# A linear-attention and MLP kernel whose first 520 entries are ordered by a written list

## The chip, the cores and the metric

The kernel runs on one core of one Trainium2 chip. The metric is device time in microseconds (us), from the start of the program to its end, as the median of several runs. A profile is one execution of it, taken by the hardware profiler.

## The reference

Two blocks follow one another. The first is linear attention with a decay per head, in blocks of 64 tokens; the second is a two-layer MLP with a leaky ReLU.

```python
batch, n_heads, seq, head_dim = (4, 8, 768, 64); block = 64
for b in range(nb):
    qb, kb, vb = (q[:, :, sl], k[:, :, sl], v[:, :, sl])
    intra = np.einsum('bhic,bhjc->bhij', qb, kb) * Dmask[None]      # lam**(i-j), lower triangle
    intra = np.einsum('bhij,bhjd->bhid', intra, vb)
    inter = np.einsum('bhid,bhde->bhie', qb * lam_pow[None], kv_state)
    out[:, :, sl] = intra + inter
    kb_dec = kb * rev_pow[None]
    kv_state = lam_block[None, :, None, None] * kv_state + np.einsum('bhsd,bhse->bhde', kb_dec, vb)
# x: (3072 tokens, 512)
h = x @ w_in            # 512 x 2048
g = np.maximum(0.01 * h, h)
return (g @ w_out).astype(np.float32)   # 2048 x 512
```

q, k, v and lam are float32. w_in and w_out are float64.

## The kernel before

**Tiling.** A chunk is 128 tokens (two blocks of 64) of one batch entry, all 8 heads; there are 24 chunks, six for each batch entry. Four chunks make a group of 512 tokens; there are six groups. The hidden width of 2048 is cut into eight units of 256. `up(g, p)` computes unit p of the first layer for group g; `down(g, p)` adds two units of the second layer.

**Precision by three products.** Every operand of the MLP is split into three fp32r parts h, l and m (`xh`, `xl`, `xm` and `wh`, `wl`, `wm`). A block of `up` is h x h products, l x l products, a scaling of the bank by ScalarE (L658), m x m products, and a leaky ReLU by ScalarE into `gs` (L661), which is stored to DRAM. Each product of 128 features is four matmuls (L640).

**float64 by hand.** `to_float32` (L566 to L585) loads half a unit of w_in as 64-bit words into one of three `raw` buffers; ScalarE makes three passes over it (L578, L580, L582), VectorE a shift (L584) and an add (L585). `parts` then makes `wh` (L591 on ScalarE or L593 on VectorE), `wl` (L596) and `wm` (L602).

**A chunk of attention.** k and q are loaded (L338) and v (L388); TensorE transposes k and q (L403); ScalarE copies the transposes out (L414, L415); k is scaled by the decay (L419, on GpSimd from chunk 2 on); q is scaled (L423, on VectorE for chunks 0 to 3, on GpSimd after); scores and the k-v products go into `psc` by quadrant matmuls (all through L313); VectorE masks the scores (L452) and updates the state (L457, L459), which GpSimd multiplies by lambda (L462); then `own` and two `inter` groups of matmuls go into `po`, with a small read of `po` between (L491), and ScalarE and VectorE split the result into `xh` (L507), `xl` (L508) and `xm` (L510).

**Order.** The functions only record operations with an engine, an assumed time and the buffers read and written (`Plan.add`). `seq` at the end of the kernel gives the rank. `Plan.emit` then simulates the engines by assumed times, takes at every step the operation that can start first, and emits all in that order. Each engine runs its own queue in order; all of the loads and stores named here are issued by SyncE. In gaps that the plan sees on TensorE before the bank `b10` is first used, `emit` calls `busy`, which adds filler transposes (L266); nine more stand at the start.

**Banks.** Four PSUM banks are used beside `psc` and `po`: `pt` for q's transposes, `b11` for k's transposes of the first four chunks, `b10` and `b2` (and later `b11`) for `up`. Which one a block of `up` gets is fixed by a counter.

## Time and profile before

| | |
|---|---|
| median of 3 runs | 610.32 us (610.25 to 611.13) |
| the profiled execution | 610.55 us |
| its span | 608.8 us |
| TensorE matmuls busy | 598.1 us |
| VectorE busy | 313.4 us |
| ScalarE busy | 269.1 us |
| GpSimd busy | 86.2 us |
| TensorE clock granted, mean | 0.999 |
| DMA read and written from HBM | 68.69 and 35.65 MB |

The span is the time from the first to the last instruction of the profiled execution; its own time is 1.75 us more. PE is TensorE's matmuls, PEld its weight loads, DVE is VectorE, ACT ScalarE, POOL GpSimd, SP SyncE. A row of a timeline gives the start, the duration, the engine, the line of the code, the operation, the output and the inputs, and the number of instructions. A row of the table by form gives the busy sum, the mean of one in ns and the idle time in front. The filler transposes count as busy.

### The profile page before, as it was taken

Reading aid. Unit: us, or ns where it says so; the run is one execution under the profiler, and the core shown is the slowest. Engines: PE = TensorE matmul, PEld = TensorE weight load, DVE = VectorE, ACT = ScalarE, POOL = GpSimd, SP = SyncE. Lnnn points to the kernel's source line nnn. Section 1 sums busy time; section 2 is a strip of 40 time slices with the busy share of each in tenths; the row PEclk is TensorE's granted clock in tenths of the full one; section 3 lists DMA queues with packets and bytes.
Section 4 is the critical chain, followed back from the end, with each engine's and each line's share of the span. In section 5 each row is a group of like instructions: output and inputs, shape, how many; then the busy total and the mean of one; then the engine's idle time right before and its main releaser. Section 6 shows DMA issues by size and latency. Waiting matters only on the chain.

```text
span 608.8 us, 12931 instructions
## 1 busy us (share of the span) xinstructions
PE 598.1 (98%) x5386; PEld 495.0 (81%) x5386; DVE 313.4 (51%) x418; ACT 269.1 (44%) x430; POOL 86.2 (14%) x90
## 2 busy tenths in 40 slices
PE   7799999999999999999999999999999999999997
PEld 6678888888888878888788888888888888888886
DVE  5899764334243426326366755545454554635531
ACT  4678974434455646555577522222222313214111
POOL 1654412105133004104000000000000000000000
PEclk9999999999999999999999999999999999999999
DMA  9999774667888878786686843524333333433201
GB/s 209 235 261 272 210 202 122 175 149 187 200 208 239 214 229 207 212 253 216 228 300 219 288 145 103 173 69 139 138 104 129 114 136 106 139 104 122 86 1 69
DMA packets 147754, 105.18 MB, mean 173 GB/s; under 512 B 123632, under 2 KB 124400, under 8 KB 147696
## 3 DMA queue, kind: packets, MB, share of 16 engines
q1 hardware_dynamic: 147408, 104.29, 58.6%
q8 instruction: 42, 0.69, 0.5%
q14 instruction: 16, 0.13, 0.1%
q10 hardware_dynamic: 288, 0.07, 0.0%
HBM read 68.69 MB, written 35.65 MB: 171 GB/s over the span
## 4 chain that ended last, share of the span: by engine, by line
PE 94%; DMA 2%; DVE 2%; ACT 1%; issue 0%; DVEq 0%; SPq 0%; ACTq 0%
PE b L640 42%; PE b L700 18%; PE po L700 11%; PE psc L700 11%; PE po L313 4%; PE psc L313 4%; PE pt L700 4%; DMA g<-gs 1%; DMA att<-in_v_dram 1%; PE pt L403 1%; DMA att<-in_k_dram 1%; PE po L403 0%; DVE wm L602 0%; ACT att L415 0%; DVE wl L596 0%; ACT gs L661 0%
## 5 line engine op out<-in xcount | busy, mean ns | idle before, releaser
L682 ACT ACTIVATE xh<-att 128x1024 fp32r<-128x1024 f32 x48 | 50.7, 1060 | 148.7 <-PE b L700 140.7
L683 DVE SCALAR_TENSOR_TENSOR xl<-att,xh 128x1024 fp32r<-128x1024 f32 x48 | 58.6, 1223 | 98.0 <-ACT xh L682 98.0
L640 PE MATMUL b<-xm,wm 128*128 128x512 f32 (+2 forms) x392 | 104.5, 392 | 0.3 <-ACT b L658 0.3
L640 PE MATMUL b<-xh,wh 128*128 128x512 f32 (+2 forms) x392 | 103.5, 387 | 0.8 <-ACT xh L507 0.8
L640 PE MATMUL b<-xl,wl 128*128 128x512 f32 (+2 forms) x392 | 103.3, 387 | 0.0
L640 PEld LDWEIGHTS b<-xh,wh 128*128 128x128 f32 x392 | 72.8, 188 | 16.5 <-ACT xh L507 0.9
L640 PEld LDWEIGHTS b<-xl,wl 128*128 128x128 f32 x392 | 72.7, 188 | 14.9 <-DVE wl L596 0.2
L640 PEld LDWEIGHTS b<-xm,wm 128*128 128x128 f32 x392 | 71.4, 188 | 15.6 <-ACT b L658 0.8
L658 ACT ACTIVATE b<-b 128x512 f32<-128x512 f32 (+2 forms) x97 | 55.9, 579 | 58.9 <-PE b L640 58.7
L661 ACT ACTIVATE gs<-b 128x512 f32<-128x512 f32 (+2 forms) x97 | 56.9, 592 | 44.5 <-PE b L640 37.9
L700 PE MATMUL b<-wh,xh 128*128 128x512 f32 x192 | 74.7, 389 | 0.0
L700 PE MATMUL b<-wl,xl 128*128 128x512 f32 x192 | 74.7, 389 | 0.0
L685 DVE SCALAR_TENSOR_TENSOR xm<-xl,xh 128x1024 fp32r<-128x1024 f32 x48 | 58.7, 1225 | 4.7
L462 POOL TENSOR_TENSOR att<-att 128x256 f32<-128x256 f32 x40 | 35.0, 874 | 57.6 <-DVE att L459 57.6
L700 PEld LDWEIGHTS b<-wl,xl 128*128 128x128 f32 x192 | 36.0, 187 | 7.5
L700 PEld LDWEIGHTS b<-wh,xh 128*128 128x128 f32 x192 | 36.1, 188 | 7.4
L452 DVE TENSOR_TENSOR att<-psc,att 128x512 f32<-128x512 f32 x24 | 16.5, 689 | 42.1 <-PE psc L313 42.0
L423 POOL TENSOR_TENSOR att<-att 128x512 f32<-128x512 f32 (+1 forms) x20 | 24.6, 1228 | 95.7 <-DVE att L383 46.8
L700 PE MATMUL psc<-wm,xm 128*128 128x512 f32 (+1 forms) x100 | 37.9, 384 | 0.0
L700 PE MATMUL psc<-wh,xh 128*128 128x512 f32 x96 | 37.3, 389 | 0.0
L700 PE MATMUL psc<-wl,xl 128*128 128x512 f32 x96 | 37.3, 389 | 0.0
L700 PE MATMUL po<-wh,xh 128*128 128x512 f32 x96 | 37.3, 389 | 0.0
(73 smaller groups left out, 784.9 us busy)
## 6 DMA issues: line engine op xcount, KB each, us to landing
att<-g SPq DMA_DIRECT2D x48, 512.0 KB, 3.2
g<-gs SPq DMA_DIRECT2D x47, 512.0 KB, 4.0
raw<-in_moe_w_in_dram SPq DMA_DIRECT2D x16, 512.0 KB, 5.1
raw<-in_moe_w_out_dram SPq DMA_DIRECT2D x16, 512.0 KB, 4.8
att<-in_k_dram SPq DMA_DIRECT2D x48, 128.0 KB, 4.1
att<-in_v_dram SPq DMA_DIRECT2D x24, 256.0 KB, 4.5
out_dram<-gs SPq DMA_DIRECT2D x23, 256.0 KB, 2.2
wo<-w SPq DMA_DIRECT2D x8, 512.0 KB, 5.7
```

The lines of the kernel that those rows point to most:

```text
L313: nc.tensor.matmul(dst[HALF[cols]], lhsT=lhsT[HALF[rows]], rhs=rhs[HALF[rows]], start=start, stop=True, skip_group_check=True)
L403: nc.tensor.transpose(out=at[y], in_=src[:, 2 * y:2 * y + 2, :].rearrange("p a d -> p (a d)"), identity=ident)
L423: add(eng, us, lambda: e.tensor_tensor(o, x, _bc(pow_q, 2, 2)[:, :, m, :], op=ALU.mult), ["fq", dep], [f"qsT{i}"])
L452: add("DVE", 0.69, lambda: nc.vector.tensor_tensor(sc, psc[:, :, lower, :], decay, op=ALU.mult), ["psc", "fk"], ["sc"])
L462: add("POOL", 0.7, lambda new=new, j=j: nc.gpsimd.tensor_tensor(state[(j + 1) % 4], new, _bc(lam_c, 2, D), op=ALU.mult), [f"st{j % 4}", "f ...
L640: nc.tensor.matmul(dst, lhsT=w[z][:, kk * 2 * P + f * P:kk * 2 * P + (f + 1) * P], rhs=x[z][:, kk, toks], start=start and kk == 0, stop=kk ...
L658: add("ACT", ns, lambda b=b: nc.scalar.activation(out=b, in_=b, func=AF.Copy, bias=0.0, scale=S + 1.0), [], [kb], rank=-1.5)
L661: add("ACT", ns, lambda b=b, r=r: nc.scalar.activation(out=r, in_=b, func=AF.Prelu, bias=0.0, scale=1.0 / WS, alpha=0.01), [kb], [f"gs{jg} ...
L682: add("ACT", 1.05, lambda: nc.scalar.activation(out=h, in_=graw[j], func=AF.Copy, bias=0.0, scale=NEAR), reads, wr("h"))
L683: add("DVE", 1.25, lambda: nc.vector.scalar_tensor_tensor(l, graw[j], 1.0, h.bitcast(F32), op0=ALU.mult, op1=ALU.subtract), reads + [f"rh{ ...
L685: add("DVE", 1.25, lambda: nc.vector.scalar_tensor_tensor(m, l.bitcast(F32), -S, h.bitcast(F32), op0=ALU.mult, op1=ALU.add), [f"rh{j}", f" ...
L700: nc.tensor.matmul((to if z == 2 else acc[tb][0])[:, cols], lhsT=ring[j][z][:, f * T + tb * P:f * T + (tb + 1) * P], rhs=W[pp][z][:, f * d ...
```

## The change

- **The list.** `ORDER` names 520 entries: an operation by its number in order of recording, and the engine that it goes to (t TensorE, s ScalarE, v VectorE, g GpSimd, d DMA). These are emitted in the listed order, and the rest by the planner as before. A negative number stands for that many fillers; there are eight of these in all, after the nine at the start, and none are added in gaps.
- **Names given late.** `Slot` objects stand for a bank, a `raw`, `low` or `gs` buffer; `Plan.resolve` gives each the free buffer of its kind that ended longest ago in the program. The banks `pt`, `b11`, `b10` and `b2` thus rotate over the transposes of k (first four chunks) and q, the k-v products of the first four chunks (which leave `psc`), and `up`.
- **q by pairs.** q of chunks 0 to 5 is loaded by three pairs of chunks; partition p holds tokens 2p and 2p+1, so that a packet is 512 bytes instead of 256. The pair is transposed by 32 matmuls of 64 x 64 into two banks; copies and scalings put the tokens back in order, the scaling of q by halves.
- **Scratch.** k, v of chunks 2 and 3 are loaded into the two `gs` buffers, q of chunks 2 and 3 into `raw2`.
- **First two units in halves.** `up(0,1)` and `up(0,0)` are each cut into chunks 0, 1 and chunks 2, 3.
- **Engines.** q's scaling is on VectorE for chunks 0 to 7, k's on either engine for chunks 0 to 7; copies of the transposes of the first four chunks may go to VectorE.
- **The planner** also gets other assumed times, and keeps VectorE's SBUF-only operations apart from GpSimd's (`lock`). `LOW_PE` and `MIX_PE` are empty, so their branches are not taken.

In recording order the entries begin with 0 to 2 the decay factors; chunk 0 is 3 to 25 (3 load k, 4 load the q pair, 5 load v, 6 and 7 transposes, 8 and 9 copies, 10 scale k, 11 scale q, 12 scores, 13 k-v, 14 mask, 15 and 17 state, 19 own, 20 and 22 inter, 23 to 25 xh, xl, xm); 26 to 47 chunk 1, 48 to 71 chunk 2, 72 to 93 chunk 3; 94 to 108 unit 1 of w_in (106 wh, 107 wl, 108 wm); 154 to 161 the first half of `up(0,1)` (159, 160 its m products); 247 wl of unit 3; 275 l products of `up(0,3)`.

```diff
+    ORDER = [(int(x[:-1]), ENGINE[x[-1]]) for x in (
+        "4d 3d -5t 7t 9s 5d 94d 26d -2t 6t 8s 12t 0v 2v 1v 14v 10g 13t 15v 11v 19t 20t 16g 96s 95s 30s 98v 17v 18g 28t 27d 31v 35t 32v 29s 21s 97s 48d 22t 23s "
+        "37v 51t 99v 33v 24v 34t 36v 41t 42t 38g 39v 25v 100d 53v 102s 101s 104v 49d 52t 43v 55g 103s 105v 54s 56v 57v 50d 163d 44t 59t 72d 73d 110d 169d 109d "
+        "58t 45s 106s 154t 40g 61v 62g 46v 60v 74t 107v 77g 65t 66t 165s 76s 75s 78v 63v 79v 155t 81t 164s 167v 82v 67s 166s 68t 69s 170s 171s 80t 156t 157t "
+        "64g 83v 84g 70v 87t 88t 113t 89s 158s 90t 91s 108v 47v 173v 85v 92v -1t 159t 160t 187t 112t 111d 225d 120d 119d 168v 115s 172s 174v 161s 114s 175s "
...
+    APART = 4
+    LOW_PE, MIX_PE = set(), set()
+    PAIRS = {"q": {0, 1, 2}}
+    QS = 8
+    KM = 8
...
+    def load_pair(nm, c):
+        b, n, i = of(c)
+        y, (dst, keys) = (q if nm == "q" else k)[b, :, n * C:(n + 2) * C, :], pair(nm, c)
+        def go():
+            for z in range(2):
+                nc.sync.dma_start(out=dst[:, z * HP:(z + 1) * HP].rearrange("p h s d -> p h (s d)"),
+                                  in_=y[z::2].rearrange("h (p s) d -> p h (s d)", s=2))
+        move(1.75, go, [], keys, issue=1.0, name=f"{nm}{c}")
...
+        def go_pair(nm, ats):
+            src = pair(nm, c)[0]
+            for y in range(HP):
+                for s in range(2):
+                    for x in range(2):
+                        for a in range(2):
+                            quad(ats[x][y][:, s * C2:(s + 1) * C2], x, src[:, 2 * y + a, s, :], ident[:, HALF[x]], a, start=y == 0 and s == 0)
...
+                for t in range(1 if n == 0 else 0, 2):
+                    add("DVE", 0.41, lambda t=t: scale_pair(t), ["fq"] + dep, [f"qsT{i}"])
...
+        kp = [Slot("bank") for _ in range(n_pu)] if apart else ["psc"] * n_pu
...
+    def resolve(self, program):
...
+                if s.name is None:
+                    able = [x for x in self.kinds[s.kind] if holds[x] is None or not holds[x].left]
+                    s.name = self.kinds[s.kind][s.fixed] if s.fixed is not None else min(able, key=lambda x: ended[x])
...
+        for i, e in self.order:
+            if i < 0:
+                done.append((free[e], len(done), i, e))
+                free[e] -= 0.11 * i
+                continue
+            take(max(free[e], since(i, e)), i, e)
...
-    seq = [("a", 0), ("a", 1), ("a", 2), ("a", 3), ("wi", 1), ("b", 4), ("r", 4), ("up", 0, 1), ("wi", 0), ("r", 5),
-           ("wi", 2), ("wi", 3), ("up", 0, 0), ("up", 0, 2), ("up", 0, 3), ("r", 6), ("up", 1, 1, 0, 3), ("r", 7),
+    seq = [("a", 0), ("a", 1), ("a", 2), ("a", 3), ("wi", 1), ("b", 4), ("r", 4), ("up", 0, 1, 0, 2), ("wi", 0), ("up", 0, 0, 0, 2), ("up", 0, 1, 2, 4), ("r", 5),
+           ("wi", 2), ("wi", 3), ("up", 0, 0, 2, 4), ("up", 0, 2), ("up", 0, 3), ("r", 6), ("up", 1, 1, 0, 3), ("r", 7),
```

## The prediction

> **What bounds the kernel now.** I read the page first: the busy shares and the chain that ended last.

> ```profile
> span 608.8 us, 12931 instructions
> ...
> PE 598.1 (98%) x5386; PEld 495.0 (81%) x5386; DVE 313.4 (51%) x418; ACT 269.1 (44%) x430; POOL 86.2 (14%) x90
> ...
> PE 94%; DMA 2%; DVE 2%; ACT 1%; issue 0%; DVEq 0%; SPq 0%; ACTq 0%
> ```

> TensorE is both the busiest engine and the chain. So the change can pay only where TensorE does nothing useful. The table by stretches shows where that is:

> ```profile
> 0.00:10.00 10.00, 7.84 (x106) 6.31 (x110) 4.94 (x21) 2.85 (x4) 1.08 (x8) 1.00 0.90 173
> 10.00:20.00 10.00, 8.18 (x264) 6.65 (x257) 7.87 (x14) 7.13 (x15) 4.56 (x6) 1.00 1.03 246
> 20.00:30.00 10.00, 7.68 (x215) 5.95 (x214) 8.58 (x13) 6.56 (x12) 6.84 (x7) 1.00 0.94 245
> 30.00:40.00 10.00, 9.54 (x104) 7.32 (x103) 9.24 (x13) 6.99 (x13) 5.84 (x5) 1.00 0.99 272
> 40.00:50.00 10.00, 10.00 (x152) 8.27 (x151) 9.62 (x14) 9.21 (x18) 3.28 (x3) 1.00 0.86 225
> ```

> Columns: stretch, length, then PE, PEld, DVE, ACT, POOL busy, granted clock, DMA share, GB/s. PE gaps end near 32 us. After that the waits of PE list only 0.34 us at 223 and 0.28 us at 298. Before it, busy PE holds fillers. DMA is full and DVE climbs to 9.6 of 10. I therefore asked which DVE operations run longer than their shortest, over 0 to 56 us by form:

> ```profile
> L585 DVE CUSTOM_DVE_ANT_0 w<-w,low 128x1024 uint16<-128x1024 uint16 x8 | 7.4, 925 | 0.6
> L584 DVE TENSOR_SCALAR w<-w 128x512 int32<-128x512 int32 x8 | 5.9, 734 | 0.0
> L596 DVE SCALAR_TENSOR_TENSOR wl<-wh,w 128x1024 fp32r<-128x1024 f32 x4 | 5.6, 1406 | 0.0
> L452 DVE TENSOR_TENSOR att<-psc,att 128x512 f32<-128x512 f32 x7 | 4.8, 688 | 2.9 <-PE psc L313 2.9
> L602 DVE SCALAR_TENSOR_TENSOR wm<-wl,wh 128x1024 fp32r<-128x1024 f32 x3 | 4.4, 1472 | 0.0
> L593 DVE TENSOR_SCALAR wh<-w 128x1024 fp32r<-128x1024 f32 x3 | 2.8, 940 | 0.1
> ```

> The forms that read only SBUF are stretched. Undisturbed rows of the same lines are 0.69 (L585, L593), 0.42 (L584) and 1.22 us (L596, L602). The excess is 1.9+2.5+0.7+0.8+0.7 = 6.6 us. L452, which reads PSUM, stays at 0.69. POOL is stretched too: L462 takes 0.62 us alone and up to 1.62.

> **A common mark.** I compare both kernels where the fourth unit, up(0,3), starts its l products. DVE's timeline has the end of the wl that it needs:

> ```profile
> 53.98 1.55 DVE L596 SCALAR_TENSOR_TENSOR wl<-wh,w 128x1024 fp32r<-128x1024 f32 x1
> ```

> and PE's the last chunk round before it and the mark itself, start and duration:

> ```profile
> 49.90 0.60 PE L403 MATMUL po<-att 128*128 128x128 f32 x4
> 50.34 0.60 PE L403 MATMUL pt<-att 128*128 128x128 f32 x4
> 50.87 0.93 PE L313 MATMUL po<-att 64*64 64x64 f32 x48
> 51.62 1.11 PE L313 MATMUL psc<-att 64*64 64x64 f32 x64
> 52.55 0.41 PE L313 MATMUL po<-att 64*64 64x64 f32 x16
> ...
> 56.65 1.98 PE L640 MATMUL b<-xl,wl 128*128 128x512 f32 x8
> ```

> From start to start these price TensorE: k and q transposes of a chunk 0.97, own and first inter 0.75, scores 0.93, second inter 0.34. A full product (4 matmuls of 512 columns) is 0.907, of 384 columns 0.70 (63.62 to 64.32); so 256 columns are 0.907 - 2 x 0.21 = 0.485, an estimate.

> DVE reaches the mark's input (end of wl for up(0,3)) at 55.53. It starts at 3.44 when lam lands. Its rows up to there, at undisturbed durations, sum to 42.3 us. So 52.1 - 42.3 = 9.8 us are lost: idle 6.5 (1.6, 2.1, 1.4, 0.8, 0.4, 0.2 by stretch), excess 6.6, less about 3.4 won because neighbours overlap (36.45 to 37.05 is 0.60 for a 0.68 us row).

> **The change, part by part.**

> *Listed order, DVE.* In the list 70 DVE entries stand up to that same wl. At the rows' durations: factors 3.2, six sc 4.1, eleven state steps 4.5, q scalings 5.2, two k scalings 1.3, eight shifts 3.4, eight adds 5.5, five xl 3.4, four xm 2.8, two heads 1.4, four wl 4.9, three wm 3.7, a copy and a peek 0.8: 44.2 us. That is 1.9 more than before, mainly q scalings that POOL had. So wl ends at 3.44 + 44.2 + loss = 47.6 + loss.

> *Loads.* Six loads of 256 KB landed from 4.55 (k of chunk 0) to 10.26 (v of chunk 1: issued 6.16, 4.1 to landing): 1.14 us each. A q pair has 512 KB in packets twice as long; no row shows these. Bounds are 1.14 (time goes by packets) and 2.28 (by bytes); I take 1.75, as w_in's 512 KB, with longer packets, lies in between. In list order this lands q of chunks 0 and 1 at 5.2, k0 6.3, v0 7.4, the first half of unit 1's w_in 9.1, k1 10.3, v1 11.4, k2 12.6, the second half 14.3. SyncE also gets the first G store ahead of the loads of unit 3's w_in. It waits for a leaky ReLU near 29; the row of such loads (6.2 us to landing at 31.81) still puts them ahead of their use near 45.

> *Walk to unit 1's third part.* k0 transposed 6.9, copied by ACT 7.6, scores 8.2; DVE idle 6.7 to 8.4. That first half's shift waits for two ACT passes (0.8 idle), the first state step for v1 and scaled k1 (0.4). With these 2.9 us (rest 0) the 21.7 us of DVE entries up to chunk 1's xm end at 28.0. Excess adds 1.2, overlap takes 1.8: 27.4. Then PE starts the m products at 27.5, against 35.38 before (there for four chunks, here for two).

> *Rest of the DVE loss.* Idle from 27 to the mark: before 1.4, take 2.0 for more joints. Excess in all: POOL had 18.8 us of work by undisturbed rows (7 k scalings of 1.06, 11 state steps of 0.62, 4.6 of q scalings) and is left 11.5, so 6.6 x 11.5/18.8 = 4.0 if the disturbance goes with POOL's work, 0 if the order avoids all; I take 2.4, nearer the row. Overlap -3.6. Sum of losses: 2.9 + 2.0 + 2.4 - 3.6 = **3.7**, bounds 0 to 9.8. [...]

> *TensorE.* A pair's q is transposed by 32 quadrant matmuls, half of the 64 in a 0.93 row: 0.47 in place of 0.97. Bounds 0.47 and 0.97. Three pairs: -1.5. Two units in halves: 24 x 0.485 - 12 x 0.907 = +0.8. From the m products to the mark the list has 22.8 us of PE work (35.8 less 13.0 by these prices). Before, 20.25 us of work took 21.27 (35.38 to 56.65), 5% more. So PE could be there at 27.5 + 22.8 x 1.05 = 51.4. DVE gives 47.6 + 3.7 = 51.3. The two agree, so neither alone yields more.

> *Fillers.* All idle fillers go but eight. They lie where PE waits, so their removal is priced at 0 while the clock holds.

> *Rotating banks, sums in a bank of their own, moved scratch.* They free waits on buffers: PE waits after 75 us are 0.6 in all, so at most 0.6 is won there, and I take 0. The greedy part after entry 520 has new costs; 0, bounds -0.6 to +2.

> *Sum.* At the mark the list has two products of 0.907 not yet done. Equal state comes at 51.4 + 1.8 = 53.2, against 56.65: 3.4 us gained. Profiled execution: 610.55 (span 608.8 and 1.75 around it), 0.23 above the median of 610.32. Forecast: 610.55 - 3.4 = 607.1 profiled, **606.9** median. In general the gain is 7.1 less DVE's loss. What 0.2% (1.2 us) can't tell from none lies between 609.1 and 611.5.

> **Rivals.**

> *Loads land sooner and the order avoids POOL.* Pair and weight halves at 1.14: v1 lands 1.2 earlier, idle falls by it, excess to 0: loss 0.1. PE is then at the m products by 25 and gives 3 more than now at most: 604. For: the entries after each state step read mostly PSUM. Against: queues drift from a plan. 0.18.

> *DVE loses what it lost before (slower).* Loss 9.8 gives 7.1 - 9.8 = -2.7: **613.0**. It decides from a loss of 7.1 up, at the mark's wl. For: more DVE entries, a fixed order that waits for its slowest load, DMA share already 1.0; and if each POOL entry blocked DVE for its whole 11.5 us, the loss would be 12.8 and the time 616.3. Against: POOL has 40% less work, and 6.6 of its 18.8 us disturbed DVE before. 0.17, of it 0.07 slower than 611.5, 0.05 within, 0.05 short of it.

> *TensorE's clock falls without fillers (slower).* The first nine fillers took 2.18 us, 0.24 each; later two take 0.44 (11.62) and five 0.76 (25.22), 0.11 for each more: a slow pace exists. About 5 us of PE steps lie on the walk; at 2.2 times they add 6: 612.9. Against: all stretches before show 1.00, with waits up to 1.4, and my walk's longest is 1.4. [...] 0.05.

> *The later, greedy part opens waits,* on banks or stores, of 2 us: 609. 0.08.

> *The list fixes order, not times:* if a pair costs 2.28, the first lands 0.5 later and the gain is 2.9; inside the forecast.

> **How the numbers follow.** Forecast 0.52 (605.2 to 608.7, loss 2 to 5.5). Faster: 0.52 + 0.18 + 0.05 + 0.04 = 0.79. Within: 0.05 + 0.03 = 0.08. Slower: 0.07 + 0.05 + 0.01 = 0.13. The range 603.2 to 610.6 leaves out the slower cases and the end of the first rival.

> **What would show it.** Right: m products of unit 1 near 27.5, wl of up(0,3) ending near 51, l products there soon after, L584 to L602 stretched by under 4 us in all before it, PE clock 1.00 from 10 us on, no PE wait over 0.5 after 75 us. Wrong: DVE idle over 5 us between 7 and 28, or PE waiting on DVE rows between 30 and 60.

## The result, and the profile after

The change is slower: 612.48 us (median of 10, 611.69 to 615.6) against 610.69 us for the kernel before beside it (10 runs, 610.17 to 612.28). The ratio is 1.0035, 95% interval 1.0018 to 1.0052. The forecast was 606.9, range 603.2 to 610.6. The profiled execution after took 614.3 us (span 612.5), 1.8 above its own median; before's took 610.55 (span 608.8).

The page of the kernel after, the busy row and the chain:

```profile
span 612.5 us, 13328 instructions
...
PE 599.5 (98%) x5589; PEld 499.9 (82%) x5589; DVE 309.2 (50%) x429; ACT 264.4 (43%) x429; POOL 77.0 (13%) x85
...
q8 instruction: 44, 0.72, 0.5%
...
PE 91%; DMA 4%; ACT 1%; issue 1%; SPq 1%; DVE 0%; DVEq 0%; ACTq 0%
```

TensorE has 203 more matmul records than before, and 4.9 us more of weight loads. The "q8 instruction" row, which I had not used, is the DMA queue that brings the instructions: 44 packets, 0.72 MB, so 16 KB each. The table by stretches, kernel after (length, PE, PEld, DVE, ACT, POOL, granted clock, DMA share, GB/s):

```profile
0.00:10.00 10.00, 7.25 (x168) 6.14 (x172) 4.15 (x20) 2.93 (x4) 1.80 (x8) 1.00 0.82 194
10.00:20.00 10.00, 6.52 (x243) 5.25 (x237) 7.35 (x16) 5.43 (x11) 4.68 (x5) 0.95 1.09 264
20.00:30.00 10.00, 8.04 (x244) 7.18 (x240) 9.27 (x17) 6.97 (x12) 3.44 (x5) 0.84 1.08 276
30.00:40.00 10.00, 10.00 (x232) 9.73 (x228) 6.13 (x9) 7.28 (x14) 1.72 (x2) 0.87 0.59 146
```

Two things stand against the rows of before. The clock is no longer 1.00, and VectorE's share at 30 to 40 us fell from 9.2 to 6.1: it waits. The timelines say for whom, first PE's, then DVE's (kernel after):

```profile
13.79 0.21 PE L428 MATMUL b<-att 64*64 64x64 f32 x1 [0.77 <-issue]
...
18.90 0.21 PE L428 MATMUL pt<-att,raw 64*64 64x64 f32 x1 [0.95 <-issue]
...
28.86 0.70 PE L871 MATMUL pt<-xl,wl 128*128 128x256 f32 x4 [1.96 <-issue]
...
32.54 0.66 PE L428 MATMUL po<-att 64*64 64x64 f32 x16
...
33.22 1.20 PE L871 MATMUL pt<-xm,wm 128*128 128x256 f32 x8
...
56.99 1.07 PE L871 MATMUL b<-xl,wl 128*128 128x512 f32 x4
```

```profile
4.05 0.24 DVE L398 COPY att<-att 128x4 f32<-128x4 f32 x2 [4.05 <-DMA att<-in_lam_dram]
...
33.87 0.69 DVE L718 TENSOR_TENSOR xl<-po,xh 128x512 fp32r<-128x512 f32 x1 [4.01 <-ACT xh L710]
...
54.33 1.23 DVE L829 SCALAR_TENSOR_TENSOR wl<-wh,w 128x1024 fp32r<-128x1024 f32 x1
```

"issue" means that the engine waited for nothing the profile shows: no buffer, no semaphore, no data. Counting all of TensorE's instructions in the trace (matmuls, weight loads and a few of its sequencer), these waits stand at instructions 450, 706 and 1218, the first two in the middle of a transposed q pair, and 450, 706, 962, 1218 are 256 apart: TensorE gets its instructions in blocks of 256 (16 KB / 256 = 64 bytes each). Its 11228 instructions pass 44 such places (194 + 256k), and the row has 44 packets; in the kernel before 10818 pass 42, with 42 packets. By the DMA records, each wait ends 1.3 to 1.4 us after the end of an instruction packet. In the kernel before the same boundaries passed at 15.36, 18.81, 24.82 and 34.47 us with no such wait, the one at 18.81 only just (1.3 us after its packet's end). VectorE then waits 4.01 us for an xh, which ScalarE makes from a chunk's output that TensorE had late (its last products started at 32.54), and the wl of up(0,3) ends at 55.56 (55.53 before), with two products of 0.907 us still to do at the mark (56.99).

### The profile page after: what moved, and what is told of

It reads as the page before. It is cut to its first block, busy times and chain, and to the rows that moved or that the text cites. A ratio compares the mean times of both kernels' runs of the same rounds, so it can differ in the third digit from the quotient of the medians.

```text
span 612.5 us, 13328 instructions
## 1 busy us (share of the span) xinstructions
PE 599.5 (98%) x5589; PEld 499.9 (82%) x5589; DVE 309.2 (50%) x429; ACT 264.4 (43%) x429; POOL 77.0 (13%) x85
## 4 chain that ended last, share of the span: by engine, by line
PE 91%; DMA 4%; ACT 1%; issue 1%; SPq 1%; DVE 0%; DVEq 0%; ACTq 0%
PE b L871 29%; PE b L938 18%; PE pt L871 11%; PE psc L938 11%; PE po L938 11%; PE po L428 4%; PE pt L938 4%; PE psc L428 3%; DMA g<-gs 2%; DMA wo<-w 1%; DMA raw<-in_moe_w_in_dram 1%; DMA raw<-in_moe_w_out_dram 1%; PE b L428 1%; PE b L564 0%; PE po L564 0%
## 5 line engine op out<-in xcount | busy, mean ns | idle before, releaser
L871 PE MATMUL b<-xm,wm 128*128 128x512 f32 (+3 forms) x296 | 77.2, 386 | 0.7 <-ACT b L896 0.7
L871 PE MATMUL b<-xh,wh 128*128 128x512 f32 (+3 forms) x296 | 76.5, 381 | 0.0
L871 PE MATMUL b<-xl,wl 128*128 128x512 f32 (+3 forms) x296 | 76.4, 380 | 0.0
L871 PEld LDWEIGHTS b<-xl,wl 128*128 128x128 f32 x296 | 54.2, 188 | 11.0 <-DVE xl L718 0.5
L871 PEld LDWEIGHTS b<-xh,wh 128*128 128x128 f32 x296 | 54.1, 188 | 10.6
L871 PEld LDWEIGHTS b<-xm,wm 128*128 128x128 f32 x296 | 52.8, 188 | 11.6 <-ACT b L896 1.3
L896 ACT ACTIVATE b<-b 128x512 f32<-128x512 f32 (+2 forms) x71 | 41.2, 581 | 41.6 <-PE b L871 41.6
L899 ACT ACTIVATE gs<-b 128x512 f32<-128x512 f32 (+1 forms) x71 | 41.6, 590 | 39.0 <-PE b L871 35.6
L655 DVE TENSOR_TENSOR att<-psc,att 128x512 f32<-128x512 f32 x24 | 16.5, 688 | 50.3 <-PE psc L428 50.2
L665 POOL TENSOR_TENSOR att<-att 128x256 f32<-128x256 f32 x40 | 29.5, 737 | 82.7 <-DVE att L662 52.3
L817 DVE TENSOR_SCALAR w<-w 128x512 int32<-128x512 int32 x32 | 15.3, 480 | 46.5 <-ACT w L811 46.5
```

The source lines that it names most:

```text
L655: add("DVE", 0.685, lambda: nc.vector.tensor_tensor(sc, psc[:, :, lower, :], decay, op=ALU.mult), ["psc", "fk"], ["sc"])
L665: add("POOL", 0.62, lambda new=new, j=j: nc.gpsimd.tensor_tensor(state[(j + 1) % 4], new, _bc(lam_c, 2, D), op=ALU.mult), [f"st{j % 4}", " ...
L817: add("DVE", 0.42, lambda: nc.vector.tensor_scalar(d, d, 3, None, op0=ALU.logical_shift_left), [], [key], lock=True)
L871: nc.tensor.matmul(dst, lhsT=w[z][:, kk * 2 * P + f * P:kk * 2 * P + (f + 1) * P], rhs=x[z][:, kk, toks], start=start and kk == 0, stop=kk ...
L896: add("ACT", ns, lambda b=b: nc.scalar.activation(out=b(), in_=b(), func=AF.Copy, bias=0.0, scale=S + 1.0), [], [kb], rank=-1.5)
L899: add("ACT", ns, lambda b=b, r=r: nc.scalar.activation(out=r(), in_=b(), func=AF.Prelu, bias=0.0, scale=1.0 / WS, alpha=0.01), [kb], [kg], ...
```

## The experiments

Every variant was timed over five rounds beside the kernel before, which had a median of 611.01 to 611.61. Numbers of the table: ratio to before with interval; start of unit 1's m products, end of the wl of up(0,3), and TensorE's waits for "issue" in the first 60 us, all three from one profiled execution, in us. Before: 35.38, 55.5, none; after: 33.22, 55.6, 3.8. In the quoted expectations S and F are one theory, that TensorE lacks its own instructions; B adds that the packets stand behind queued data. C is the halved clock in e1 to e7; in e9 to e11 it is that a packet takes a time of its own.

| run | ratio (95%) | m products | wl end | issue |
|---|---|---|---|---|
| e1 no pairs | 1.0029 (1.0017 to 1.0041) | 31.9 | 54.1 | 0.2 |
| e5 no pairs, 26 fillers | 1.0026 (1.0010 to 1.0043) | 28.7 | 51.0 | 2.9 |
| e17 the same again | 1.0026 (1.0010 to 1.0042) | 30.3 | 52.5 | 2.3 |
| e6 pairs, 26 fillers | 1.0053 (1.0036 to 1.0070) | 35.8 | 58.1 | 6.7 |
| e9 e5, q of chunk 8 later | 1.0007 (0.9992 to 1.0021) | 28.9 | 51.6 | 2.7 |
| e10 e9, store ahead of W4 | 1.0009 (0.9996 to 1.0022) | 29.9 | 52.7 | 1.8 |
| e11 e10, W4 held | 1.0029 (1.0014 to 1.0043) | 29.6 | 51.7 | 1.4 |
| e12 one pair (4, 5), 26 fillers | 0.9998 (0.9982 to 1.0014) | 29.9 | 52.3 | 1.5 |
| e15 the same again | 1.0019 (1.0005 to 1.0033) | 32.1 | 55.3 | 2.2 |
| e13 e12 with e10's loads | 1.0030 (1.0013 to 1.0048) | 31.5 | 53.8 | 2.6 |
| e16 the same again | 1.0040 (1.0014 to 1.0066) | 32.9 | 56.3 | 2.8 |
| e14 one pair (0, 1), 26 fillers | 1.0018 (1.0004 to 1.0032) | 32.4 | 56.1 | 1.9 |

**No pairs (e1).**

```diff
-    PAIRS = {"q": {0, 1, 2}}
+    PAIRS = {"q": set()}
```

with the list's numbers moved to match; the two q loads of a pair stand where the pair's stood.

> The changed kernel with q of chunks 0 to 5 loaded, transposed and scaled chunk by chunk again, each entry at its place in the list: 24 matmuls in place of 96 for these transposes, so 144 fewer TensorE instructions (a weight load and a matmul each). Theory S (TensorE waits for its own instructions, which come in blocks of 256, about 5 us apart in the first 30 us): the waits at 13.8, 18.9 and 28.9 us shrink or vanish, 610.5 to 611.7, that is 0.8 to 2 faster than the change. Theory L (the pair loads with longer packets are what helps the start): every early load is later, 613.5 to 615. Theory C (only the halved clock costs): within 0.5 of the change, unless the clock also stays up.

The instruction waits are gone (0.2 us), but the time stayed near the change's (1.0029 against 1.0035), so theory S missed its gain of 0.8 to 2 us. The run has 168 matmul records fewer, 336 instructions with their weight loads and not 144. The granted clock fell instead (10 to 20 us, then 20 to 30, kernel e1):

```profile
10.00:20.00 10.00, 7.72 (x168) 5.99 (x160) 6.81 (x15) 5.56 (x10) 4.68 (x5) 0.65 0.90 220
20.00:30.00 10.00, 9.71 (x278) 8.42 (x280) 7.54 (x13) 7.00 (x12) 3.80 (x4) 0.84 1.02 231
```

**Long fillers (e2).** Three fillers of 512 columns were listed at two waits of the change.

```diff
+        if n > 100:
+            for _ in range(n - 100):
+                nc.tensor.matmul(bank[at][:, 0:T], lhsT=ident, rhs=_bc(ident, 1, 4), start=True, stop=True, skip_group_check=True)
+            return
```

> The changed kernel with three more fillers of few instructions: one matmul of 512 columns ahead of chunk 1's own products (where TensorE waits from 15.6 to 16.5 us) and two ahead of the l product that starts at 28.9 us. They keep TensorE busy in both 3.4 us windows that came before a half-speed window, with 6 more instructions. Theory C: no half-speed window up to 60 us, time 610.8 to 611.6. Theory S: the instruction waits stay, though the clock holds: 612 to 613 (gain under 0.5).

614.37, ratio 1.0045 (1.0029 to 1.0062). The fillers did not fill this wait, being instructions too: two of them came right behind the 1.98 us wait at 28.13 and held the next products up by 2.5 us (28.36 to 30.87). Of the two slow stretches of the clock the first was gone and the second stayed (from 28.48 us); the time lay above both forecasts.

**No list (e3), and neither list nor pairs (e8).** ORDER is empty, so the planner orders all and adds its own fillers.

> The changed kernel with an empty list: pairs, halves and rotating banks stay, and the planner orders everything and adds its own fillers in gaps. Theory O (the listed order itself is what loses, or what wins): off from 612.5 by over 2 either way. Theory S: the planner's fillers take more instructions, the blocks come late as well, 612 to 615. Theory C: fillers hold the clock at 1.00, so 611 or less if nothing else matters.

> The changed kernel with an empty list (planner orders all and adds its fillers) and without the pairs; halves, rotating banks and new costs stay. With pairs this took 7 us more than before and its profile had waits for instructions of 2.6, 0.6, 1.7 and 1.3 us at TensorE's instructions 451, 963, 1218 and 1474. Theory S: these vanish, 3 to 5 us faster than with pairs. Rival: pairs only cost the list's slack, within 1 us of it.

618.63 (1.0119, 1.0094 to 1.0144) and 620.88 (1.0147, 1.0114 to 1.0180). The list itself is thus worth some 5 us on the rest of the change. That the pairs' absence would help here was a miss. The planner's order has instruction waits of its own (e3: 6.4 us in the first 60); without pairs they shrank to 3.6 us in e8, and that brought no time.

**Many small fillers in the kernel before (e4).** Each planned filler became four float32 matmuls of 32 columns.

> The kernel before, each of its 22 idle fillers (one transpose of 128 columns) replaced by four matmuls of 32 columns: about the same busy time, off every data path, 132 more TensorE instructions before 28 us. Theory S: a block of 256 is used up earlier each time, waits for instructions appear; 611.3 to 613 (0.6 to 2.5 slower than before). Theory C: same activity, no change (610.3 to 611.0).

The ratio is 1.0386 (1.0356 to 1.0417). The edit was mis-sized: a 32-column matmul took some 0.2 us (24 of them 5.17), with weight loads of 186 to 337 ns, so this is added work, and it tells nothing of the blocks.

**The fillers back (e5 without pairs, e6 with).** Before list entries 12, 19, 35, 41 and 65 stand `-5t -2t -9t -6t -4t`.

> The kernel of the run without pairs (its profile: no instruction wait over 0.2 us, but 10.2 us at half clock from 13.1 us on), with 26 more fillers of 128 columns placed where its TensorE waits (5 before chunk 0's scores, 2 before its own products, 9 before chunk 1's k-v products, 6 and 4 before the own products of chunks 1 and 2). Theory C (with the instruction waits gone, the half clock is what remains): clock 1.00 to 60 us, 1.5 to 3 us faster than without them, so at or below the kernel before. Theory D (the start is bound by loads and VectorE whatever the clock): within 0.7 of the run without pairs.

> The changed kernel, pairs kept, with the same 26 fillers at the same places. Theory S (instructions come late because a 64 x 64 float32 matmul is two matmul records and two weight loads, so a pair costs 128 TensorE instructions against 16): the fillers use up 52 more instructions, the waits for instructions stay or grow; 612 to 614, no gain. Theory C: clock 1.00, 1 to 2.5 us faster than the change.

These two are the same but for the pairs. Stretches of 20 to 40 us, e5, then e6:

```profile
20.00:30.00 10.00, 9.30 (x239) 7.92 (x233) 8.60 (x16) 7.34 (x15) 3.97 (x5) 1.00 1.13 261
30.00:40.00 10.00, 9.94 (x219) 9.35 (x221) 9.86 (x15) 8.93 (x16) 3.63 (x4) 1.00 1.05 254
```

```profile
20.00:30.00 10.00, 6.98 (x246) 6.24 (x242) 5.96 (x11) 7.04 (x12) 2.81 (x3) 0.89 0.98 238
30.00:40.00 10.00, 8.23 (x231) 7.62 (x234) 7.03 (x13) 4.84 (x9) 1.24 (x2) 1.00 0.67 171
```

Without pairs VectorE's chain is where it was forecast (wl at 51.0, forecast 51.3). With them it is 7.1 later, and PE waits 6.7 us for instructions. But e5 is no faster than e1, though its clock held: its theory C missed and D came true. It gives the gain back on TensorE, where the quadrant blocks of a round use up a block (PE, kernel e5):

```profile
51.22 0.21 PE L429 MATMUL psc<-att 64*64 64x64 f32 x1 [2.14 <-issue]
...
55.82 1.07 PE L872 MATMUL b<-xl,wl 128*128 128x512 f32 x4
```

With 0.83 us at 44.26 that is 3.0 us of instruction waits without any pair. The second row is the mark, again with two products to do: the equal state comes at 57.6, 1.0 later than before, although the wl came 4.5 earlier.

**No fillers in the kernel before (e7).** `plan.idle` is None.

> The kernel before without its idle fillers (the nine at the start stay). Theory C: half-speed windows appear between 10 and 35 us, 1 to 3 us slower than before. If the clock stays at 1.00 or the time within 0.5: fillers are worth nothing and Theory C falls.

612.11, ratio 1.0011 (0.9997 to 1.0025); its clock at 10 to 40 us was 0.83, 0.89 and 0.77. So the fillers are worth at most 0.25%, and 0 is not excluded. Without them the order of the kernel before has an instruction wait too, 1.07 us at 26.45.

**Does queued data delay the packet (e9, e10, e11)?** On e5 the loads of W4 and of chunks 7 and 8 were moved. e9: q of chunk 8 listed behind k of chunk 8. e10: also the store of the first half of G ahead of W4's first load. e11: also

```diff
+    gate = dram.tile([1, P], F32, name="gate", tag="gate")
...
+            if (kind, p, h) == ("wi", 4, 0):
+                nc.sync.dma_start(out=gate, in_=W[2][2][0:1, 0:P].bitcast(F32))
```

so that SP's queue waits for wm of unit 2 ahead of W4.

> The kernel is the fifth run (no token pairs, 26 fillers back); one load moves: q of chunk 8, which stood at 40.85 us on the queue, is listed behind k of chunk 8 (some 49 us). Theory B (TensorE's blocks of 256 instructions stand behind the data already queued for the DMA engines): the packet for the boundary at 44.3 us starts sooner after its boundary only if less data is queued then, and here W4's loads now start some 3 us sooner instead, so the packet that started 3.5 us after the boundary at 38.5 us stays as late (W3's 1 MB is still ahead of it) and the one after that is still 3 us or more late; the waits at 44.3 (0.8 us) and 51.2 (2.1 us) together shrink by less than 1 us; about 613. Rival theory C (a packet takes a time of its own, whatever data is queued): both waits as before, within 0.3 us; about 613.

> As the run beside it, and the first load of W4 (512 KB) also waits for the end of unit 2's middle part (45.6 to 46.8 us in the fifth run), with the store of the first gate half ahead of it; so next to no data is queued when the block of TensorE instructions of the boundary at 44.3 us is fetched. Theory B: that packet starts within 2 us of its boundary instead of 4.5, the 2.1 us wait at 51.2 is gone, and the kernel gains 1 to 2 us on the fifth run, less what W4's later arrival (2 to 3 us) costs VectorE, which waited 1.9 us for it at 55.9 already: 611 to 613. Theory C: the packet starts 4 us or more after its boundary, the wait stays at 2 us, and the kernel is 613 to 614.

> The tenth run only moved the loads of W4 behind the store of the first gate half (they started at 45.6 us, and the instruction packet 3.7 us after its boundary at 45.8), so it did not put the question. Here a copy of 512 bytes of unit 2's finished middle part (done at 47 to 48 us) stands ahead of the first W4 load on SP's queue, so W4, v of chunk 7 and k of chunk 8 start behind it, at 48 us. Theory B (TensorE's blocks of 256 instructions wait behind the data already queued): with only a 256 KB store queued at the boundary near 45.8 us, the packet starts within 2 us of it, before 48 us, and the wait of 1.3 us at 52 is gone; W4 comes 2 to 3 us later and VectorE waits that much longer for it near 56; in total 611 to 613, within 0.2% of the tenth run. Theory C (a packet takes its own time, whatever data is queued): it starts 3.5 us or more after the boundary and the wait at 52 stays over 1 us.

The packet fetched from instruction 1730 on, needed at 1986, started 4.5 us after that boundary in e5 (4.9 in e17), 3.1 in e9, 3.7 in e10 and 1.9 in e11; the wait at 1986 was 2.1 (2.3), 1.4, 1.3 and 0. In e10 W4 started with the store, at 45.6 us, so the extra wait that its expectation names did not come about. In e11 the first W4 load was issued at 47.9 and the packet started then. PE, kernel e11, at the same instructions (55 records into psc, then po without a wait):

```profile
49.79 1.09 PE L430 MATMUL psc<-att 64*64 64x64 f32 x55
50.68 0.28 PE L430 MATMUL po<-att 64*64 64x64 f32 x3
```

While the packet was late, the DMA share was 0.93 in e5, 0.89 in e17 and e9, 0.79 in e10 and 0.36 in e11. So theory B has this boundary and C does not, on one execution of each kernel. Queued data is not all of what sets the delay: over the 154 boundaries passed in the first 60 us of all traces but e4's, the packet's delay has a median of 1.4 us where under 0.4 MB of loads and stores were issued and not yet moved, and 2.6 where it was 0.6 MB or more, with single delays up to 6.5 us in the first group and 4.0 in the second. Holding W4 back brought no time: the one wait left in e11 was 1.4 us at the boundary before, behind W3's 1 MB, and q of chunk 8 was now late (0.88 us at 62.70).

**A third of the pairs (e12, e14), and loads on top (e13).** `PAIRS = {"q": {2}}`, then `{"q": {0}}`; e13 is e12 with e10's order of loads.

> The sixth run (the change with 26 fillers back) with only chunks 4 and 5 as a token pair: a third of the extra TensorE instructions (112 of 336). Theory F (the pairs cost by their instructions, which come in blocks of 256): instruction waits in the first 40 us between the fifth run's (none over 0.5 us) and the sixth's (6.7 us), some 1 to 3 us, and the fourth weight unit's low part between 51.0 and 58.1 us, about 53; total between the two, 613 to 614. Rival L (the pairs cost by their loads and layout, not by instructions): the waits at every 256th instruction stay under 0.5 us, as in the fifth run, and the fourth low part is at 51 or late for another reason, a wait for data or VectorE.

> The sixth run with only chunks 0 and 1 as a token pair: as many extra TensorE instructions as in the twelfth, but in the first 10 us, where the list runs its blocks of quadrant matmuls earliest. Theory F: every later boundary of 256 instructions comes at work that is 112 instructions earlier from the first block on; total instruction waits in the first 56 us between the fifth run's 3 us and the sixth's 6.7, placed at the same instruction numbers 194 + 256k; fourth low part 52 to 55; 611 to 614. Rival P (only the place of the boundaries against the dense blocks counts, and this one is shifted as in the twelfth from 24 us on): waits of 1.5 us or less in all after 24 us, as in the twelfth run, and 610 to 611.

> The twelfth run (token pair for chunks 4 and 5 only, 26 fillers) with the load order of the tenth: q of chunk 8 behind k of chunk 8, the store of the first gate half ahead of W4. The fifth run gained about 1.3 us by that order (1.0026 to 1.0008 of before). Theory F with B: the twelfth run has no instruction wait in 40 to 56 us left for the order to save, so it brings nothing there, and the kernel is within 0.2% of the twelfth, 610 to 612, with the one wait of 1.5 us near 29 us still there. Rival O (the load order itself was worth the 1.3 us, by data or buffers): 1 us or more faster than the twelfth, under 610.

e12's wl and its wait in the first 40 us lie between those of e5 and e6, as theory F has it, but its time (610.78) does not, and its profiled span of 607.7 us is the shortest of all. e14, with as many extra instructions but earlier, has its wl 3.8 us later, and missed both its theories: its waits are under F's 3 us and over P's 1.5, its wl (56.1) is behind F's 55, its time (612.31) over P's 611. e13 missed both of its theories: its median is 2.3 us above e12's, which was taken on another chip. So the last runs put three kernels on one chip.

> The twelfth run's kernel once more, beside the thirteenth's and the fifth's on one chip. Theory F: the three differ only by where TensorE's instruction blocks fall; this one keeps the best place, 0.9985 to 1.0010 of before. Rival Z (the spread between the variants is the spread between visits, 2 us from launch to launch, and says nothing on the order): the three lie within 0.1% of each other.

> The thirteenth run's kernel once more. Theory F: within 0.15% of the run beside it (its load order differs only after 36 us, where that kernel has no instruction wait), so the 0.3% between the twelfth and thirteenth does not come back. Rival G (the load order costs: q of chunk 8 behind k of chunk 8 makes TensorE wait for it at 62 us, 1.2 us in the thirteenth's trace): 0.2% or more slower than the run beside it, with that wait in the trace again.

> The fifth run's kernel (no pairs, 26 fillers) once more. Theory F: slower than the twelfth's by the instruction waits near 44 and 51 us (0.8 and 2.1 us in the fifth run's trace, none there in the twelfth's): 1.5 to 3 us, and those waits are in the trace again. Rival Z: the same time within 0.1%.

The medians were 612.77, 612.91 and 612.69: within 0.04%, rival Z; their ratios (1.0019, 1.0040, 1.0026) spread by 0.2%, with intervals that overlap. Behind that lies one kernel that ran in two ways. PE, then DVE, of e12, and the same of e15:

```profile
29.07 0.62 PE L429 MATMUL b<-att 64*64 64x64 f32 x26 [1.54 <-issue]
51.07 1.23 DVE L830 SCALAR_TENSOR_TENSOR wl<-wh,w 128x1024 fp32r<-128x1024 f32 x1
```

```profile
30.64 1.01 PE L429 MATMUL b<-att 64*64 64x64 f32 x26 [2.17 <-issue]
54.06 1.23 DVE L830 SCALAR_TENSOR_TENSOR wl<-wh,w 128x1024 fp32r<-128x1024 f32 x1
```

The packet for instruction 1218 started 2.1 us after its boundary in e12 and 3.0 in e15; the wait was 0.6 longer, the clock fell to half for 3.41 us behind it (26 records in 1.01 us instead of 0.62), wl came 3.0 later and the span was 3.0 longer (610.7). The waits come back at the same instruction numbers (e17: 2.27 us at 1986 again); their size changes from one execution to the next. One profile therefore can't tell e14's place from e12's, and the steps of 0.1 to 0.2% between e9 to e16 carry no weight; e6 against e5 and e17 (58.1 against 51.0 and 52.5) does. No variant beats the kernel before. Open is why a packet's delay differs by 0.9 us (2.1 and 3.0) between executions of one kernel.

## Why the prediction was wrong

- **Which step failed: "Rest of the DVE loss" and "Walk to unit 1's third part", the idle time.** Forecast 2.9 + 2.0 = 4.9 us; the trace has 10.0 up to the wl of up(0,3), of it 4.0 at one row (33.87), for which TensorE was late, and 0.6 because lam landed at 4.05 instead of 3.44. The walk priced TensorE's steps by busy rows alone, and its instructions as free. m products were due at 27.5 and came at 33.22; 3.7 of these 5.7 us are the three instruction waits. The rest, about 2.0, was not split: the slow clock is part of it, but not shown to be all. e5, with no such wait up to there and the clock at 1.00, has its m products at 28.7, still 1.2 late, and its wl at 51.0. No run shows the whole stretch without instruction waits and without a slow clock: in e5 3.0 us of waits stand behind the m products, where the walk had priced instructions at nothing too.
- **"32 quadrant matmuls ... 0.47".** A float32 quadrant product is two matmul records and two weight loads (the three pairs have 168 matmul records more than the 24 transposes that they replace: 192 for 96 products), so a row of "x64" is 32 of them, and a pair costs a whole row of 0.93, next to the 0.97 it replaces. The 1.5 us that I gave it do not exist. Its price is elsewhere: 128 instructions instead of 16, for three pairs 336, more than one block, in a stretch where the packets started at 11.1, 16.4, 20.9 and 26.2 us (kernel after), about 5 us apart.
- **DVE's list and excess** held: the rows sum to 44.9 us without their excess (44.2 forecast), the excess is 2.4 (2.4 forecast, 6.6 before; L829's four rows take 1223 ns each), beside a POOL that is busy 14.5 us up to there (25.7 before). Overlap won 5.1 and not 3.6, so the loss is 10.0 + 2.4 - 5.1 = 7.3 against 3.7: idle time adds 5.1 and the overlap takes 1.5 back. (The row sum of before, by the same count, is 43.4 and not 42.3, its loss 8.7 and not 9.8.)
- **From the m products to the mark** 23.8 us against 22.8 x 1.05 = 23.9. The walk behind the failed step was right.
- **Sum.** Mark at 56.99, two products still to do: equal state at 58.8, 2.15 later than before instead of 3.4 sooner. That gives 612.7, and the median is 612.48; the profiled execution lost 1.6 us more later. Its waits there are 0.2, 0.7 and 0.3 us at 226, 270 and 297 (0.3 at 223 and at 298 before), so most of this is not accounted for. The greedy part's 0 is about right where the rows show it: e5 is 1.0 late at the mark and its span 0.6 longer than before's, e12 1.5 early (mark at 53.33) and 1.1 shorter.
- **Fillers priced at 0 "while the clock holds".** It did not hold: 0.50 at 20 to 22 and 30 to 32 us. The rival of the clock named this with 6 us. The slow stretches were real, but e6, fillers back and pairs kept, gained nothing, since the instruction waits grew to 6.7.
- **The rival "DVE loses what it lost before" gave 613.0**, nearest to the result, with the right place (that wl) and the wrong mechanism: it blamed slow loads and POOL, and the largest part of VectorE's loss was TensorE's. That VectorE is blocked for all of GpSimd's time (its 616.3) is not shown: the excess was 2.4 us.
- **The two signs of being wrong** that I had named did not come: VectorE was idle 4.8 us between 7 and 28 (over 5 was the sign), and TensorE waited for no VectorE row between 30 and 60. The signs looked for a late VectorE, and the wait ran the other way. "PE clock 1.00 from 10 us on", a sign of being right, failed.

The halves of the first two units were not tried by themselves.

## What to carry to other kernels

Count instructions, not only busy time: e6 has 336 TensorE instructions more than e5, its instruction waits in the first 60 us were 6.7 us against 2.9, and its wl came 7.1 us later. Look for "issue" waits at equal steps of the engine's instruction count (256 here), and for the instruction queue's packets beside them. Loads that are issued earlier than needed may delay the instructions that should use them; one boundary here shows it (its packet started 4.5 us behind it with W4's loads issued, 1.9 with them held back), and no time came of moving them.

## What the runs showed of the hardware

```profile
28.00:30.00 2.00, 1.14 (x23) 0.93 (x26) 1.86 (x4) 0.00 (x0) 0.06 (x1) 0.82 1.19 272
30.00:32.00 2.00, 2.00 (x84) 2.00 (x83) 0.00 (x0) 0.65 (x2) 0.56 (x1) 0.50 0.26 49
```
